# Shorter ways for the softmax sums and the heads' rows, two more score blocks and a new written-out order in a gated attention and mixer block

## The chip, the core and the metric

The kernel runs on one core of a Trainium2 chip. A core has a matrix engine (TensorE, PE in the profile; its weight loads, PEld, are listed apart), a vector engine (VectorE, DVE), a scalar engine that evaluates functions (ScalarE, ACT), a general engine (GpSimd, POOL), and a synchronising engine (SyncE, SP), on whose queue nearly all DMA transfers of this kernel are issued. The metric is the time of one execution in microseconds on the device.

## The reference, cut to what matters

There are 2048 tokens of 512 features. `a` is attention with 32 heads of 16 features and no mask; `b` is a mixer with a shift of the hidden rows and a wide MLP; a gate of each token mixes the two.

```python
g = _sigmoid((x * gate_w).sum(-1, keepdims=True))
qkv = (x @ wqkv).reshape(B, S, 3, H, Dh)          # H = 32, Dh = 16
p = _softmax(einsum(q, k) * (Dh ** -0.5))
a = einsum(p, v).reshape(B, S, D) @ wo
h = _gelu(_layernorm(x) @ w1)                     # quarters of h shifted by 1, -1, 2, -2 tokens
x1 = x + shifted(h) @ w2
b = x1 + _gelu(_layernorm(x1) @ w3) @ w4          # w3: 512 x 1792
return g * a + (1 - g) * b
```

All inputs are bf16. The largest part is the attention: 32 x 2048 x 2048 exponentials.

## The kernel before, in words

**Blocks and rounds.** The 2048 queries are cut into 4 chunks `c` of 512. The 32 heads are 4 groups `G` of 8; of these, 4 heads lie in the 4 row quarters of PE at once, the even ones in the first round (`p` = 0) and the odd ones in the second. So there are 4 x 4 x 2 = 32 rounds (`rounds`, L1497), each with 16 key tiles x 4 heads = 64 score blocks of 128 keys x 512 queries, 2048 blocks in all. A block is one matmul on a quarter of PE (L1536) into one of the 8 PSUM banks.

**Two ways to take an exponential.** Either ACT evaluates Exp on 2 or 3 blocks at once (L1631) and writes `prob`; or DVE does it on pairs of blocks. DVE multiplies and adds so that the 16 bits of the result, read as bf16, are a rough exponential (L1663), and then adds 32, 64 and 96 to these bits (`sh`, L1704): the four versions together give a good one. The additions run on DVE (L1706) or on POOL (L1708). A block of ACT's needs one value matmul (L1761), a block of DVE's four. The value matmuls have a column of ones beside the 16 value features, so that row 0 of each quarter of the sum is the softmax's denominator. `prob` has room for 56 blocks (`NPROB`, L908).

**End of a round.** `finish_round` (L1772) copies the sum to `accsb` (DVE, L1782), then sends its four rows of denominators to DRAM (`den`, L1784) and from there to `pk`, 16 to a partition (L1786), takes the reciprocal, multiplies by the gate's factor (L1789, L1790), writes it to DRAM (`rr`, L1792), and reads it back to all partitions in four transfers (`bcs`, L1796). POOL multiplies (`oT`, L1800). Four transfers then put the 16 rows of each head at their place in the group's buffer `oD` (L1804), in which both rounds of a group lie together. `oD` has 6 buffers of 512 columns, `oT` two. The matmuls with `wo` (loaded in one piece, L1091) run at the end of the MLP's last product (`w4`, L1447 to L1455). The very last round is finished apart, behind L2122.

**MLP.** Its products run between the score blocks in groups of column quarters (`gen`, L1127). A normalised tile is made on POOL (L1358), stored to DRAM (`xn_dram`, L1362) and read back transposed (L1368).

**The start.** x's first four tiles come on two queues, then the first query weights (`wq`, L1051) on SP and the first key weights on ACT's queue, then x's second chunk in one piece of 512 KB (L1053), the first value weights (L1054), and transposed chunks of x (L1060). PE warms up with 9 matmuls, transposes the first chunk (L1206) and projects it (L1198); the second chunk is transposed on PE later (L1165).

**What sets the order.** Nothing is scheduled on the chip. The class `Sim` runs a model of the five engines while the kernel is built: each step is a `Job` with a duration (`hold`), a latency, dependencies, buffers that it takes and frees, and a priority; SP's transfers are jobs too (`dma`, L1009). The times at which the model starts the jobs give the order in which the instructions are written out (L2116), and each engine then follows that order and waits on semaphores. Its choices depend on some 40 settings, `BASE`, that a table `STEPS` overwrites for each stretch of 8 score blocks, 256 stretches in all. Some of them: `GP2`, the share of DVE's pairs that have two additions on POOL and not one; `GP3`, one minus the share of pairs with all three on DVE; `DVE_WAIT`, how many blocks may wait for DVE; `DVE_STOP`, at how many blocks left in a round DVE gets no more; `CAP3`, up to how many banks ACT's blocks may hold for three to be taken together.

Of the kernel before, what the change touches and what calls it, by code (L numbers as in the profile page):

```python
# [191 lines left out]
class Sim:  # L192
# [6 lines left out]
    def __init__(self, slots):  # L199
# [24 lines left out]
        self.readers = {}  # L224
        self.usable = [0.0] * 8
# [108 lines left out]
    def try_engine(self, e):  # L334
# [136 lines left out]
def kernel(  # L471
# [77 lines left out]
        0: dict(P1_PRIO=0.312, GP2=0.15, DVE_STOP=8, DVE_STOP_L=12, DVE_ALONE=138, SL0=-150, SL1=130, IDLE_NS=864,  # L549
            BRES=2, AHEAD=16, PV_FULL=0.947, PV_IDLE=0.25, PRESS=22, ROT=1, AT_SH=118, HOLE=3, CAP3=5, LIMD=4, GATE=4,  # L550
            AFIRST=1, LIMA=2, JOIN=1),
        1: dict(P1_PRIO=0.743, S_PRIO=0.178, DVE_STOP_L=7, URG=2, DVE_ALONE=-158, SL0=45, SL1=0, PV_IDLE=0.731,
            E_PRIO=0.25, JOIN=2),
        2: dict(ROT=3, E_PRIO=2, ROWM=7),
        3: dict(P1_PRIO=0.414, S_PRIO=0.625, GP2=0.8, DVE_STOP_L=16, URG=3, DVE_ALONE=2, SL0=0, B_LOW=5, DVE_WAIT=2,
            AHEAD=24, AHEAD2=32, PV_IDLE=0.5, MAXU=3, DUE_SH=-6, AT_SH=69, MAXG=2, CAP3=0, LIMD=3, GATE=3, E_PRIO=0.25,
            AGE=6000, ROWM=3, JOIN=0),
        4: dict(GP2=1, EARLY=64, SL1=-150),
        5: dict(P1_PRIO=0.743, S_PRIO=0.3, DVE_STOP=2, DVE_STOP_L=7, URG_L=18, DVE_ALONE=362, SL1=60, B_LOW=8, BRES=4,
            AHEAD2=24, PV_FULL=0.916, PV_IDLE=0.25, PRESS=18, MAXU=2, ROT=2, HOLE=7, MAXG=1, CAP2=5, CAP3=7, AFIRST=2,  # L560
            AGE=9000, ROWM=99, LIMA=3),
        6: dict(P1_PRIO=0.312, S_PRIO=0.214, DVE_STOP=13, DVE_STOP_L=16, URG_L=12, DVE_ALONE=2, B_LOW=3, BRES=0,
            DVE_WAIT=1, AHEAD2=32, PV_FULL=1, PV_IDLE=0.117, ROT=0, DUE_SH=-14, HOLE=0, MAXG=3, GATE=4, AFIRST=1,
            AGE=3000, JOIN=1),
        7: dict(S_PRIO=0.38, E_PRIO=2, AGE=12000),
# [620 lines left out]
    def first(t):  # L1186
# [45 lines left out]
        for k in range(KT):  # L1232
            j_xT[0, 0, k] = at_time(t + 2100.0)
# [538 lines left out]
    def finish_round(r):  # L1772
# [35 lines left out]
        if r == NR - 2:  # L1808
            packs.extend(d4)
# [366 lines left out]
```

## Time and profile before

| | |
|---|---|
| median of 3 runs | 731.45 us (731.16 to 733.74) |
| the profiled execution | 731.34 us, of which the span of instructions is 729.4 |
| granted clock of TensorE | 1.0 |
| busy: PE, DVE, ACT, POOL | 719.9, 698.0, 713.2, 481.0 us |
| DMA | 38.27 MB, mean 52 GB/s |

How to read a group: line of the kernel, engine, operation, tile written <- tile read, shapes, count | busy time in us, mean duration in ns | idle time of the engine just before, and what ended it. Durations of neighbours overlap on an engine, so that the busy time of a group is less than count x mean. A row of a stretch has its two ends, then for PE, PEld, DVE, ACT and POOL the busy us with the number of instructions in brackets, the first figure being the stretch's length. A row of one line of the kernel gives the shortest, median and longest duration in ns and the first and last start. In a list of waits there are the waiting engine and line, what it waited for, the us in total, how often, and the longest.

### The profile page before, as it was taken

How to read it: one execution, taken by the hardware profiler on the slowest of the kernel's cores; microseconds unless marked ns; L12 is line 12 of the kernel's file. 1: busy time of each engine (PE TensorE's matmuls, PEld its weight loads, DVE VectorE, ACT ScalarE, POOL GpSimd, SP SyncE). 2: the span in 40 equal slices, each digit the busy share in tenths (PEclk: the TensorE clock that was granted, in tenths of full speed). 3: DMA queues.
4: the chain of work that ended last, by engine and by line, in shares of the span. 5: the costliest groups of instructions: out<-in, count | busy, mean ns of one | idle time of the engine just before them, and what ended most of it. 6: DMA issues, size and time to landing. Idle time of an engine off the chain costs nothing.

```text
span 729.4 us, 23745 instructions
## 1 busy us (share of the span) xinstructions
PE 719.9 (99%) x9533; PEld 214.3 (29%) x9533; DVE 698.0 (96%) x1461; ACT 713.2 (98%) x728; POOL 481.0 (66%) x502
## 2 busy tenths in 40 slices
PE   9999999999999999999999999999999999999997
PEld 5334322232332222223222222222222232222222
DVE  6999899999999999999999999999999999999997
ACT  6999989999999999999999999999999999999995
POOL 2786767778786876685556556686777856564451
PEclk9999999999999999999999999999999999999999
DMA  9222422323123210141111101221100131000001
GB/s 188 79 61 54 101 71 46 65 50 89 61 67 79 59 41 22 45 137 53 24 26 35 28 22 29 63 80 28 41 19 21 36 102 26 25 28 21 18 19 40
DMA packets 69543, 38.27 MB, mean 52 GB/s; under 512 B 46893, under 2 KB 64317, under 8 KB 69433
## 3 DMA queue, kind: packets, MB, share of 16 engines
q1 hardware_dynamic: 68472, 36.23, 19.7%
q8 instruction: 74, 1.21, 0.7%
q10 hardware_dynamic: 960, 0.52, 0.3%
q14 instruction: 37, 0.29, 0.2%
HBM read 21.07 MB, written 6.81 MB: 38 GB/s over the span
## 4 chain that ended last, share of the span: by engine, by line
PE 80%; ACT 13%; DVE 2%; issue 2%; DMA 1%; POOL 1%; SPq 0%; ACTq 0%; DVEq 0%
PE banks L1761 29%; PE banks L1536 26%; PE banks L1134 24%; ACT prob L1631 12%; ACT hT L1378 1%; DVE prob L1706 1%; DMA wq<-in_A_wqkv_dram 1%; DMA xn_dram<-xn 1%; DVE prob L1663 0%; PE banks L2111 0%; POOL prob L1708 0%; ACT L1378 0%; DVE hB L1431 0%; PE banks L1291 0%; PE banks L1198 0%
## 5 line engine op out<-in xcount | busy, mean ns | idle before, releaser
L1631 ACT ACTIVATE prob<-banks 128x1024 bf16<-128x1024 f32 (+1 forms) x705 | 669.1, 1121 | 3.1 <-PE banks L1536 2.8
L1708 POOL TENSOR_SCALAR prob<-prob 128x1024 uint16<-128x1024 uint16 x364 | 374.5, 1047 | 180.7 <-DVE prob L1706 118.5
L1663 DVE TENSOR_SCALAR prob<-banks 128x512 uint16<-128x512 f32 (+1 forms) x577 | 385.0, 693 | 12.7 <-PE banks L1536 8.0
L1761 PE MATMUL banks<-prob,V 128*17 128x512 bf16 (+1 forms) x3818 | 319.6, 381 | 2.1 <-POOL prob L1708 1.5
L1536 PE MATMUL banks<-q,kT 32*128 32x512 bf16 x2048 | 275.7, 384 | 1.4 <-ACT prob L1631 0.2
L1706 DVE TENSOR_SCALAR prob<-prob 128x1024 uint16<-128x1024 uint16 x521 | 192.3, 423 | 3.6 <-POOL prob L1708 2.3
L1536 PEld LDWEIGHTS <-kT 32*128 32x128 bf16 x2048 | 69.1, 90 | 289.0 <-ACT prob L1631 265.5
L1761 PEld LDWEIGHTS <-V 128*17 128x17 bf16 (+1 forms) x3818 | 73.5, 88 | 120.0 <-issue 96.4
L1134 PE MATMUL banks<-xnT,w 128*32 128x512 bf16 x1152 | 92.1, 383 | 0.0
L1800 POOL TENSOR_TENSOR oT<-accsb,bcs 128x512 bf16<-128x512 f32 x31 | 39.5, 1275 | 28.8 <-DVE prob L1706 24.8
L1134 PE MATMUL banks<-w,hT 128*32 128x512 bf16 x696 | 57.6, 383 | 0.0
L1134 PEld LDWEIGHTS <-w 128*32 128x32 bf16 x1904 | 40.3, 95 | 48.3 <-issue 28.1
L1134 PE MATMUL banks<-w,w 128*32 128x256 bf16 (+1 forms) x752 | 38.0, 309 | 0.0
L1134 PE MATMUL banks<-w,hB 128*32 128x512 bf16 x448 | 37.7, 382 | 0.0
L1358 POOL TENSOR_SCALAR xn<-x_sb,rs,nm 128x512 bf16<-128x512 bf16 x32 | 25.0, 785 | 13.8 <-DVE prob L1706 3.7
L1145 PE MATMUL banks<-w,oD 32*128 32x512 bf16 x56 | 21.5, 384 | 0.0
L1338 DVE BATCH_NORM_STATS2 st<-x_sb 128x6 f32<-128x512 bf16 x32 | 21.4, 680 | 0.0
L1782 DVE COPY accsb<-banks 128x512 f32<-128x512 f32 x31 | 21.1, 680 | 0.1
L1134 PE MATMUL banks<-w,oD 128*32 128x512 bf16 x184 | 21.0, 384 | 0.1
L1134 PEld LDWEIGHTS <-hT 128*32 128x32 bf16 x696 | 14.9, 95 | 19.9 <-issue 14.0
L1134 PE MATMUL banks<-w,wq 128*32 128x512 bf16 x240 | 19.8, 383 | 0.0
L1378 ACT ACTIVATE hT<-hT 128x7168 bf16<-128x7168 bf16 (+1 forms) x3 | 19.4, 6452 | 0.0
(100 smaller groups left out, 273.6 us busy)
## 6 DMA issues: line engine op xcount, KB each, us to landing
bcs<-rr SPq DMA_DIRECT2D x124, 64.0 KB
xn_dram<-xn SPq DMA_DIRECT2D x32, 128.0 KB
w<-in_B_w_dram SPq DMA_DIRECT2D x8, 512.0 KB
w<-in_B_w_dram SPq DMA_DIRECT2D x8, 448.0 KB
oD<-oT SPq DMA_DIRECT2D x124, 16.0 KB
x_sb<-in_A_x_dram SPq DMA_DIRECT2D x3, 512.0 KB
out_dram<-ot SPq DMA_DIRECT2D x12, 128.0 KB
w<-in_A_wqkv_dram SPq DMA_DIRECT2D x2, 256.0 KB
```

Source lines behind the costliest of these rows:

```text
L1134: units.append([Op("col", j, lambda j=j, lf=lf, rf=rf, n0=n0, n1=n1, st=st, sp=sp: nc.tensor.matmul(get()[32 * j:32 * j + 32, n0:n1], lhsT ...
L1145: o = Op("row", i, lambda: nc.tensor.matmul(get(), lhsT=lf(0, P)[rows], rhs=rf()[rows], start=False, stop=True, tile_position=(32 * i, 0), ...
L1338: a = dve(600, deps, lambda: nc.vector.bn_stats(out=sb.slot[:], in_=x_sb[:, t, :]), prio=6, at=at, acq=[sb])
L1358: g = gp(750, [m], lambda t=t, xb=xb: nc.gpsimd.tensor_scalar(out=xb.slot[:], in0=x_sb[:, t, :], scalar1=rs[which][:, t:t + 1], scalar2=nm ...
L1378: g = nc.scalar.activation(out=ap, in_=ap, func=ACT.Gelu_apprx_tanh)
L1536: o = Op("row", i, lambda: nc.tensor.matmul(dst(), lhsT=kT[G][32 * i:32 * i + 32, kt * P:(kt + 1) * P], rhs=qbuf[G, c].slot[32 * i:32 * i ...
L1631: job = act(hold, ops, lambda: nc.scalar.activation(out=prob[:, pb.cut(), :].bitcast(BF16), in_=unit()[:, rb.cut(), :], func=ACT.Exp, scal ...
L1663: return nc.vector.tensor_scalar(out=prob[:, b0.cut() if w == 2 else b0.bufs[h0].slot, :], in0=unit()[:, rb.cut() if w == 2 else rb.bufs[0 ...
L1706: return nc.vector.tensor_scalar(out=cut(k), in0=cut(0), scalar1=float(SHIFT * k), scalar2=None, op0=ALU.add)
L1708: return nc.gpsimd.tensor_scalar(out=cut(k), in0=cut(0 if both else 2), scalar1=1.0, scalar2=float(SHIFT * (k if both else 1)), op0=ALU.mu ...
L1761: return nc.tensor.matmul(one(accs[r])[32 * i:32 * i + n, :], lhsT=lhs(n), rhs=rhs(), start=st and not edge, stop=True, tile_position=(0, ...
L1800: n = gp(1250, d3, lambda: nc.gpsimd.tensor_tensor(out=ob.slot[:], in0=ab.slot[:], in1=bb.slot[:], op=ALU.mult), acq=[ob], frees=[ab, bb], ...
```

## The change

- The row sums go from `accsb` to `pk` in one transfer within SBUF; `den` is gone.
- Of each round but the last two, `oT` is stored whole, in one transfer of 128 KB, to a new DRAM array `o_dram`. When both rounds of a group are stored, one load brings the group's 128 rows of heads into `oD`. `oD` has four buffers and not six. The round before the last keeps its four direct transfers, with other places.
- In `oD` the even heads' rows now lie ahead of the odd ones', and `wo` is loaded in eight pieces so that its rows have the same order.
- `prob` has room for 58 blocks.
- x's second chunk on SP waits for the landing of the first query weights. All later transfers of the start stand behind it on that queue.
- One warm-up matmul fewer; two of the start's copies change between ACT and DVE.
- The model holds SP back while eight transfers are in flight (`sent`), and some of its durations are other ones.
- The whole table `STEPS` is a new one, so that the order of all engines is new. Over the 256 stretches the mean of `GP2` goes from 0.537 to 0.562, of `GP3` from 0.863 to 0.856, of `DVE_WAIT` from 3.00 to 2.67, of `DVE_STOP` from 7.37 to 6.52, of `CAP3` from 1.63 to 1.29.

```diff
@@ class Sim
+        self.sent = [0.0] * 8
...
+            land = max(self.t + 0.65 * (j.hold + j.lat), min(end, self.queue + 1500.0))
+            self.sent = self.sent[1:] + [land]
+            if self.sent[0] > self.t_free[e]:
+                self.t_free[e] = self.sent[0]
+                self.push(self.t_free[e], None)
@@ STEPS
-        0: dict(P1_PRIO=0.312, GP2=0.15, DVE_STOP=8, DVE_STOP_L=12, DVE_ALONE=138, SL0=-150, SL1=130, IDLE_NS=864,
...
+        0: dict(P1_PRIO=0.1, S_PRIO=0.214, GP2=0.8, DVE_STOP=8, URG_L=18, DVE_ALONE=500, SL0=0, SL1=130, IDLE_NS=864,
...
-    NPROB, NTOK, NW = 56, 5, 6
+    NPROB, NTOK, NW = 58, 5, 6
...
+    o_dram = dpool.tile([4 * NCH, 2, P, 512], BF16, name="o_dram")
...
-        "oD": slots("oD", 6, [P, 512]),
+        "oD": slots("oD", 4, [P, 512]),
...
-        "den": slots("den", 3, [4, 512], F32, dpool),
...
-        fn(nc.sync if eng == "SP" else nc.scalar)
+        insts.append(fn(nc.sync if eng == "SP" else nc.scalar))
         return job
+
+    insts = []
+
+    def behind(inst, first):
+        tc.add_manual_dep(inst.ins, first.ins.name, mybir.DependencyInfo(
+            mybir.DependencyClass.Sync, mybir.DependencyReason.DATA), reason="load order")
...
-    j_x1 = [start("SP", 4900.0, lambda q: q.dma_start(out=x_sb[:, 4:8, :], in_=x_src(1, 0, 4)))]
+    issue["SP"] = 5400.0
+    j_x1 = [start("SP", 2900.0, lambda q: q.dma_start(out=x_sb[:, 4:8, :], in_=x_src(1, 0, 4)))]
+    behind(insts[-1], insts[4])
...
-    wload("o", A_wo, 10 ** 6)
-    dl_w["o"].at = 855
+    bo = wslot("o", 10 ** 6)
+    for n in range(8):
+        G, p = n // 2, n % 2
+        dl_w["o"] = dma(3000.0, [], lambda G=G, p=p: nc.sync.dma_start(
+            out=bo.slot[64 * p:64 * p + 64, G, :],
+            in_=A_wo[G * P:(G + 1) * P, :].rearrange("(j p i) c -> p j i c", p=2, i=16)[p]), acq=[] if n else [bo], prio=2)
...
-        for _ in range(9):
+        for _ in range(8):
...
-                cp = nc.scalar.copy if i in (1, 3) else nc.vector.tensor_copy
+                cp = nc.scalar.copy if i == 2 else nc.vector.tensor_copy
...
-            sim.readers[ba] = [nc.vector.tensor_copy(out=kT[0][:, 0:256], in_=one(ba)[:, 0:256])]
+            sim.readers[ba] = [nc.scalar.copy(out=kT[0][:, 0:256], in_=one(ba)[:, 0:256])]
...
-                in_=zE_dram[S - 512:S].rearrange("(b e) -> e b", e=32)), prio=6)
+                in_=zE_dram[S - 512:S].rearrange("(b e) -> e b", e=32)), prio=6).at = 300 + 20 * j
...
-            wdeps = [dl_w["o"]] + j_att[c][:2 * ng]
+            wdeps = [dl_w["o"]] + j_att[c][:ng]
...
+        for G in range(4 if c < NCH - 1 else 3):
+            j_att[c].append(dma(3300.0, [att_done[c * 8 + 2 * G], att_done[c * 8 + 2 * G + 1]], lambda c=c, G=G: nc.sync.dma_start(
+                out=oDbuf[c, G].slot[:], in_=o_dram[4 * c + G].rearrange("p (j q) n -> (p j) q n", q=32)[:, 1:DH + 1, :]),
+                acq=[oDbuf[c, G]], prio=1))
...
-        d0 = dma(2000.0, [e], lambda: nc.sync.dma_start(out=db.slot[:], in_=ab.slot[0:P:32, :]), prio=1, acq=[db],
-                 frees=[ab], hold=580.0)
-        d1 = dma(2800.0, [d0], lambda: nc.sync.dma_start(
-            out=kb.slot[:], in_=db.slot[:].rearrange("j (b e) -> (j b) e", e=16)), prio=1, acq=[kb], frees=[db],
-            hold=400.0)
+        d1 = dma(2600.0, [e], lambda: nc.sync.dma_start(out=kb.slot[:], in_=ab.slot[0:P:32, :]), prio=1, acq=[kb],
+                 frees=[ab], hold=570.0)
...
+        fin = Call(lambda: sim.set_done(att_done[r]))
+        if r < NR - 2:
+            dma(2900.0, [n], lambda: nc.sync.dma_start(out=o_dram[4 * c + G, p], in_=ob.slot[:]), frees=[ob, fin], prio=1,
+                hold=400.0)
+            return
         d4 = []
         for j in range(4):
...
-                out=oDbuf[c, G].slot[32 * j + 16 * p:32 * j + 16 * p + 16, :], in_=ob.slot[32 * j + 1:32 * j + DH + 1, :]),
...
+                out=oDbuf[c, G].slot[64 * p + 16 * j:64 * p + 16 * j + 16, :], in_=ob.slot[32 * j + 1:32 * j + DH + 1, :]),
```

More of the change, by code (lines that the diff above doesn't have):

```diff
@@ L558 @@
[L558 to L564, printed above, removed]
@@ L1833 @@
             PLAN["w4", 4 * c + t] = int(a + (b - a) * t / 4)
[L1835 removed]
+    first(3480.0)
     begun = [j_ka[0], j_q[0, 0, 0]]
```

730 lines of the change are left out of this document (366 added, 364 removed).

## The prediction

> **What bounds the kernel now.** I read the page's busy shares and its chain first, then the groups by shape, then busy time by stretch, and last the timeline of the one stretch that stands out. The busy shares:
>
> ```profile
> PE 719.9 (99%) x9533; PEld 214.3 (29%) x9533; DVE 698.0 (96%) x1461; ACT 713.2 (98%) x728; POOL 481.0 (66%) x502
> PE 80%; ACT 13%; DVE 2%; issue 2%; DMA 1%; POOL 1%; SPq 0%; ACTq 0%; DVEq 0%
> ```
>
> Three engines look full. The stretches tell them apart (columns: time, then busy us and instructions of PE, weight loads, DVE, ACT, POOL, the granted clock, the DMA share, GB/s):
>
> ```profile
> 0.00:10.00 10.00, 8.26 (x63) 5.53 (x63) 4.32 (x13) 4.51 (x7) 3.88 (x14) 1.00 0.92 195
> 60.00:88.00 28.00, 28.00 (x488) 10.89 (x484) 27.04 (x57) 28.00 (x29) 18.99 (x22) 1.00 0.40 90
> 88.00:90.00 2.00, 1.55 (x26) 0.31 (x15) 0.44 (x2) 2.00 (x3) 2.00 (x3) 1.00 0.13 42
> 90.00:94.00 4.00, 2.92 (x35) 0.94 (x34) 2.46 (x10) 2.24 (x3) 0.86 (x2) 1.00 0.20 55
> 94.00:120.00 26.00, 25.90 (x342) 7.10 (x340) 25.20 (x47) 25.33 (x28) 22.28 (x24) 1.00 0.20 55
> 94.00:715.00 621.00, 619.45 (x8046) 173.76 (x8047) 606.40 (x1250) 619.93 (x634) 418.51 (x425) 1.00 0.17 46
> 360.00:480.00 120.00, 119.88 (x1556) 31.43 (x1547) 117.98 (x250) 119.98 (x132) 73.69 (x73) 1.00 0.15 42
> 715.00:730.00 15.00, 10.07 (x93) 3.23 (x86) 8.92 (x20) 6.81 (x9) 1.57 (x2) 1.00 0.12 40
> ```
>
> From 94 to 715 us ACT is idle 1.07 us in 621 and DVE 14.6. So there is no repeated wait to remove: ACT's exponentials are the bound, and DVE, which takes part of the score blocks off ACT, has 2.4% left. ACT's idle time lies at the start (5.5 us of the first 10), at the end (8.2 from 715 on), and in one place between: 1.76 us in 90 to 94 and 0.67 in 94 to 120, 2.43 together, with 3.1 us of DVE's in 88 to 94. All of ACT's from 88 to 715 is 1.76 + 1.07 = 2.83.
>
> The division of the score blocks, by shape (count, then busy time and mean duration):
>
> ```profile
> L1631 ACT ACTIVATE prob<-banks 128x1024 bf16<-128x1024 f32 x657 | 614.0, 1089 | 2.9 <-PE banks L1536 2.7
> L1631 ACT ACTIVATE prob<-banks 128x1536 bf16<-128x1536 f32 x48 | 74.0, 1550 | 0.2 <-PE banks L1536 0.2
> L1708 POOL TENSOR_SCALAR prob<-prob 128x1024 uint16<-128x1024 uint16 x364 | 374.5, 1047 | 180.7 <-DVE prob L1706 118.5 <-PE banks L1761 20.8 <-PE banks L1536 13.2
> L1663 DVE TENSOR_SCALAR prob<-banks 128x512 uint16<-128x512 f32 x564 | 369.5, 681 | 12.2 <-PE banks L1536 7.7 <-issue 0.3 <-PE banks L1761 0.2
> L1706 DVE TENSOR_SCALAR prob<-prob 128x1024 uint16<-128x1024 uint16 x521 | 192.3, 423 | 3.6 <-POOL prob L1708 2.3 <-PE banks L1761 0.4 <-DVE prob L1706 0.2
> L1663 DVE TENSOR_SCALAR prob<-banks 128x1024 uint16<-128x1024 f32 x13 | 15.9, 1220 | 0.5 <-PE banks L1536 0.3
> ```
>
> ACT does 657x2 + 48x3 = 1458 blocks, DVE 564 + 26 = 590, together the 2048. A block on ACT costs 688.0/1458 = 0.47 us. A pair on DVE costs 2 x 385.4/590 = 1.31 us and its shifts: 521 + 364 = 885 = 3 x 295, so 1.77 of three on DVE at 192.3/521 = 0.37 us, 0.65 together. One pair moved from ACT to DVE thus frees ACT 0.94 us and costs DVE 1.96.
>
> **The change, part by part.** The terms are summed against the profiled execution, 731.34 us (span 729.4), which stands 0.11 under the median of the runs, 731.45.
>
> *Start.* x's second chunk (512 KB on SP) now waits until the first query weights have landed, and everything behind it on SP waits too.
>
> ```profile
> 1.68 4.56 DMA wq<-in_A_wqkv_dram
> 2.17 0.58 SPq L1053 DMA_DIRECT2D x_sb<-in_A_x_dram  x1
> 3.97 1.91 PE L1206 MATMUL banks<-idb,x_sb 128*128 128x128 bf16 x16
> 6.28 0.61 PE L1198 MATMUL banks<-w,wq 128*128 128x256 bf16 x4 [0.39 <-DMA wq<-in_A_wqkv_dram]
> 8.78 5.97 ACT L1631 ACTIVATE prob<-banks 128x1536 bf16<-128x1536 f32 x5 [0.17 <-PE banks L1536]
> 9.13 1.07 PE L1165 MATMUL banks<-idb,x_sb 128*128 128x128 bf16 x16
> ```
>
> PE ends the transposes at 5.88 and starts projecting at 6.28, after 0.39 us of waiting for the weights. That wait is all that a faster landing can give. I take half, -0.2, as the weights still share the DMA engines with the first key weights. The other end: the chunk is issued at 6.24 instead of 2.17; with a flight as long as the weights' 4.56 it lands at 6.24 + 0.58 + 4.56 = 11.4, while PE transposes it from 9.13. PE takes its work in order, so the scores behind would be late by 2.3; ACT's five exponentials, 5.97 us from 8.78, cover most of that. Ends -0.4 and +2.3. One warm-up matmul fewer and the copies moved between ACT and DVE end before the weights' landing, or in place of one another: nothing.
>
> *Row sums and heads' rows.* Per round, two hops of the sums become one and four transfers of the rows become one; per pair of rounds one load is added.
>
> ```profile
> L1784 SPq DMA_DIRECT2D den<-accsb x31: 499/532/1032, 38.6 to 701.8; - x31
> L1786 SPq DMA_DIRECT2D pk<-den x31: 326/341/576, 40.4 to 703.5; - x31
> L1804 SPq DMA_DIRECT2D oD<-oT x124: 508/587/1626, 79.6 to 717.4; - x124
> L1134 PE MATMUL banks<-w,oD x184: 376/379/392, 330.5 to 716.6; 128*32 128x512 bf16 x184
> ```
>
> Removed are 31 hops and 30 x 3 row transfers, added 15 loads and 7 for the split output weights: 99 transfers fewer. By these rows SP issues for about 31 x 0.34 + 90 x 0.59 - 22 x 0.59 = 50 us less, and a round's reciprocal can come 40.4 - 38.6 = 1.8 us sooner. The rows now make a trip to DRAM and back, two flights of some 4.2 us for one. What hides both is the distance of the output projection, which in before starts only at 330 us for rows finished from 80 us on. With four buffers for them instead of six, a finished chunk waits in DRAM and holds no oT. So away from the stall below I cost these at nothing; uncovered, the added flight is 4.2 us a chunk. The last pair keeps its four direct stores, so the end is unchanged.
>
> *The stall at 88 to 94 us.* Its timeline and the chain there:
>
> ```profile
> 83.40 4.17 DMA xn_dram<-xn
> 84.47 2.41 SPq L1804 DMA_DIRECT2D oD<-oT  x4
> 86.98 0.54 SPq L1784 DMA_DIRECT2D den<-accsb  x1
> 87.66 2.02 POOL L1358 TENSOR_SCALAR xn<-x_sb,rs,nm 128x512 bf16<-128x512 bf16 x2 [1.15 <-DMA xn_dram<-xn]
> 89.65 1.04 POOL L1708 TENSOR_SCALAR prob<-prob 128x1024 uint16<-128x1024 uint16 x1
> 90.73 0.43 DVE L1706 TENSOR_SCALAR prob<-prob 128x1024 uint16<-128x1024 uint16 x1 [2.29 <-POOL prob L1708]
> 91.97 0.25 DVE L1789 RECIPROCAL pk<-pk 128x16 f32<-128x16 f32 x1 [0.81 <-DMA pk<-den]
> ```
>
> POOL's normalisation waits for a store in flight; the shift queued behind it on POOL is late; DVE waits 2.29 us for that and then 0.81 for a row sum's second hop; PE and ACT follow. Both transfers that bracket it are in the part that is cut, and the planner now also holds SP back when eight transfers are in flight, so a new order would place such stores where they come in time. I take the whole of ACT's loss here, -2.4. The other end is a second stall of that size, +2.4: it is the only one in 705 us, and a new order can have its own. Late next is the gate's own chain, which does not change.
>
> *Two more score blocks, new settings.* The order of all five engines is planned anew. Averaged over the 256 stretches of the table (each setting holds until it is overwritten), GP2, the share of pairs with a second shift on POOL, goes from 0.537 to 0.562, and GP3, one minus the share with all on DVE, from 0.863 to 0.856. Shifts on DVE per pair, 3(1 - GP3) + GP3(2 - GP2), fall from 1.67 to 1.66: 0.011 x 295 x 0.37 = 1.2 us less on DVE, of which 0.94/(0.94 + 1.96) reaches the time: -0.4; I take -0.3. By the Trainium skill's page SBUF — State Buffer, Who interferes with whom, a GpSimd instruction and a DVE one in a two-port mode exclude each other on a shared port pair, which speaks against this term; the trace agrees as far as POOL's 118.5 us of waiting on L1706 goes, and by the rule the sum would be 0.3 higher.
>
> For the rest: DVE has 14.6 us in 94 to 715, and used up entirely that is 14.6/(1.96 + 0.94) = 5.0 pairs, 4.7 us. I take the row of 360 to 480, where the same planner leaves DVE 1.7% idle: with that everywhere, 10.5 us would be left, so 4.1/2.90 x 0.94 = -1.3. Ends -4.7 and zero, or worse if the new order is the poorer one (below). Width of the exponentials: CAP3, which allows three blocks, falls from 1.63 to 1.29 on average; 0.51 us a block busy in the wide ones against 0.47 says a gain, 0.52 against 0.54 by duration a loss; nothing taken.
>
> Sum: 731.34 - 0.2 - 2.4 - 0.3 - 1.3 = 727.1; against the median, 727.2.
>
> **Rivals.** *A: no change.* The stall comes back as a similar one, and the new order packs no better; only the start and the shifts are left, 731.45 - 0.2 - 0.3 = 730.9. For it: outside the stall ACT has 0.4 us of idle time from 88 to 715 to give back, and the removed transfers end no other wait. Against it: DVE's spare 14.6 us.
>
> *B: slower, by the division of work.* The new order gives DVE fewer pairs. DVE_WAIT, the blocks that may wait for DVE, falls from 3.00 to 2.67 on average, and DVE starves wherever a block comes late, with ACT doing the rest at 0.94 us a pair. Ten pairs of the 295 cost 9.4: 727.2 + 9.4 = 736.6. It decides at 4.5 pairs; slower by 0.5% begins at 8.4. Against it: DVE_STOP, the rest of a round at which DVE gets no more, falls too (7.4 to 6.5), which gives DVE more.
>
> *C: PE bounds.* If PE's 80% of the chain were its own work, pairs moved to DVE, which need eight matmuls after the exponential where ACT's need two, would cost instead of help, and the -1.3 goes: 728.5. Against it: before 640 of the scores' groups the weight loads wait for ACT, 265.5 us in all.
>
> ```profile
> PEld L1536 <- ACT prob L1631: 265.5, 640, 0.6
> ```
>
> By the Trainium skill's page Perfetto Trace Analysis, Identifying the Most-Contended Engine, matmul busy time is a poor measure of how full PE is, and the weight loads' share a better one. The trace agrees, with 29% beside 99%; by that rule C falls away.
>
> **How the numbers follow.** 0.5% of the time, 3.7 us, is about what a measurement tells from no change: faster is below 727.8, slower above 735.1. The forecast has 0.50, with a range of its own from 723.5 to 729.5, of which 0.41 lies below 727.8; all bounds of gain together give 731.45 - 0.4 - 2.4 - 0.4 - 4.7 = 723.5. A has 0.16. C has 0.07, of which 0.03 is below 727.8. B has 0.27, of which 0.25 is over 735.1 and some 0.10 over 737.5, since lost pairs add up with a second stall or the late chunk. So faster 0.44, same 0.31, slower 0.25. The range from 723 to 737.5 leaves out about 0.05 below and 0.10 above.
>
> **What would show it.** Start: PE's first projection waits under 0.2 us for wq, and the first exponential starts by 8.6; wrong if the transposes of the second chunk wait for x_sb. Stall: ACT's idle time between 88 and 715 us falls from 2.83 to under 1; wrong if POOL's normalisation still waits for xn_dram. Division: 296 to 298 pairs, shifts on DVE at or below 1.77 a pair, DVE idle 10 us; with fewer than 291 pairs B holds. Rows: the output projection waits for no oD load, and accsb's copy for no buffer. The prediction is wrong above all if ACT has as little idle time as I say and more than 1458 blocks.

## The result, and the profile after

The changed kernel takes 728.49 us (median of 8 runs, 727.93 to 730.26), the kernel before 731.77 beside it (8 runs, 729.75 to 733.74): a ratio of 0.9956, with a 95% interval of 0.9941 to 0.9971. That is 3.3 us less, just inside the 0.5% that the prediction called no change. The profiled execution took 728.68 us, its span 725.9; before, 731.34 and 729.4. So the span fell by 3.5 us and the time by 2.7: what lies outside the span grew from 1.94 to 2.78.

The busy shares of the changed kernel, from its page:

```profile
PE 716.5 (99%) x9560; PEld 215.2 (30%) x9561; DVE 700.4 (96%) x1467; ACT 712.8 (98%) x729; POOL 478.4 (66%) x501
```

Busy time by stretch after, with the columns of the prediction's (PE, weight loads, DVE, ACT, POOL, granted clock, DMA share, GB/s):

```profile
0.00:10.00 10.00, 7.97 (x58) 5.02 (x59) 5.09 (x14) 5.44 (x8) 3.87 (x14) 1.00 0.62 171
10.00:60.00 50.00, 49.62 (x829) 20.40 (x830) 48.55 (x112) 49.10 (x47) 34.48 (x39) 1.00 0.39 96
88.00:94.00 6.00, 5.88 (x96) 2.01 (x88) 6.00 (x16) 5.90 (x8) 1.73 (x3) 1.00 0.20 51
94.00:120.00 26.00, 25.82 (x349) 7.33 (x345) 25.08 (x50) 26.00 (x29) 20.05 (x21) 1.00 0.25 50
94.00:712.00 618.00, 615.44 (x8036) 174.16 (x8032) 603.67 (x1245) 617.55 (x635) 415.87 (x422) 1.00 0.19 51
```

The one stall is gone: ACT loses 0.10 us in 88 to 94 and nothing in 94 to 120; before, it lost 2.43 in the two together. From 94 to 712 it loses 0.45 us in all. Something came in, though. From 10 to 60 ACT loses 0.90 us. Before, the same stretch reads so:

```profile
10.00:60.00 50.00, 49.69 (x808) 19.67 (x809) 48.40 (x114) 49.75 (x49) 35.14 (x39) 1.00 0.39 83
```

That was a loss of 0.25. The groups by shape after (count, then busy time and mean duration, then idle time before):

```profile
L1652 ACT ACTIVATE prob<-banks 128x1024 bf16<-128x1024 f32 x659 | 614.5, 1096 | 0.4
L1652 ACT ACTIVATE prob<-banks 128x1536 bf16<-128x1536 f32 x47 | 72.4, 1540 | 1.1 <-PE banks L1557 1.1
```

and DVE's and POOL's:

```profile
L1684 DVE TENSOR_SCALAR prob<-banks 128x512 uint16<-128x512 f32 x575 | 375.9, 681 | 11.9 <-PE banks L1557 7.0
L1684 DVE TENSOR_SCALAR prob<-banks 128x1024 uint16<-128x1024 f32 x7 | 8.5, 1219 | 0.4 <-PE banks L1557 0.3
L1727 DVE TENSOR_SCALAR prob<-prob 128x1024 uint16<-128x1024 uint16 x519 | 192.2, 425 | 2.2 <-PE banks L1782 1.3 <-issue 0.2 <-PE banks L1557 0.2
L1727 DVE TENSOR_SCALAR prob<-prob 128x512 uint16<-128x512 uint16 x3 | 0.7, 288 | 0.0
L1729 POOL TENSOR_SCALAR prob<-prob 128x1024 uint16<-128x1024 uint16 x363 | 372.7, 1045 | 187.8 <-DVE prob L1727 131.3 <-PE banks L1782 16.1 <-PE banks L1557 11.7
```

ACT does 659 x 2 + 47 x 3 = 1459 blocks (1458 before), DVE 575 + 7 x 2 = 589 (590 before). The 589 are 294 pairs and one block alone, which has its three shifts on DVE at half the width. The shifts are 519 + 3 + 363 = 885, as before, and 522 of them are on DVE (521 before), that is 1.77 of three, as before. The division of the work has moved by one block.

The start and the end, from the timeline after:

```profile
5.28 0.38 SPq L1064 DMA_DIRECT2D x_sb<-in_A_x_dram  x1
5.31 0.61 PE L1216 MATMUL banks<-w,wq 128*128 128x256 bf16 x4
7.81 3.71 ACT L1652 ACTIVATE prob<-banks 128x1536 bf16<-128x1536 f32 x3 [0.17 <-PE banks L1557]
9.64 1.07 PE L1183 MATMUL banks<-idb,x_sb 128*128 128x128 bf16 x16
711.54 6.02 ACT L1652 ACTIVATE prob<-banks 128x1536 bf16<-128x1536 f32 x5
718.04 0.72 DVE L2140 STREAM_TRANSPOSE accsb<-banks 128x512 f32<-128x512 f32 x1
```

and the end before:

```profile
708.90 11.64 ACT L1631 ACTIVATE prob<-banks 128x1536 bf16<-128x1536 f32 x12
719.78 1.05 POOL L1708 TENSOR_SCALAR prob<-prob 128x1024 uint16<-128x1024 uint16 x1 [4.25 <-ACT prob L1631]
721.50 0.72 DVE L2122 STREAM_TRANSPOSE accsb<-banks 128x512 f32<-128x512 f32 x1 [1.60 <-PE banks L1761]
```

The first exponential starts at 7.81 and not at 8.78, since PE's first projection starts at 5.31 and not at 6.28; from there to the exponential it takes 2.50 us in both. The last exponential ends at 711.54 + 6.02 = 717.56, and 8.34 us of the span follow; before it ended at 720.54, with 8.86 us behind it. There the last pair's shift on POOL (1.05 us) is still to come when ACT is nearly done, and the closing transposition waits 1.60 us; in the new order that shift runs on DVE and the transposition waits for nothing.

So the 3.5 us of span are made up of: first exponential earlier, 0.97; shorter tail, 0.52; ACT's idle time between 88 us and the end of the score blocks down from 2.83 to 0.10 + 0.45 = 0.55, 2.28; and against these 0.65 more of idle time from 10 to 60. That makes 3.12. The other 0.38 is ACT's own work (its busy time fell from 713.2 to 712.8) and rounding. Outside the span 0.84 is lost again. This compares one execution with one; a second execution of the changed program, told of at the end of the experiments, has its first exponential at 8.14.

One wait of the old stall is still there, in small:

```profile
POOL xn L1376 <- DMA xn_dram<-xn: 0.8, 2, 0.5
```

POOL's normalisation waits twice for a store, at 75 and at 83 us, and ACT loses nothing there (it is busy for all 28 us from 60 to 88).

### The profile page after: what moved, and what is told of

The parts are those of the page before. It is cut to its first block, busy times and chain, and to the rows that moved or that the text cites. A ratio compares the mean times of both kernels' runs of the same rounds, so it can differ in the third digit from the quotient of the medians.

```text
span 725.9 us, 23600 instructions
## 1 busy us (share of the span) xinstructions
PE 716.5 (99%) x9560; PEld 215.2 (30%) x9561; DVE 700.4 (96%) x1467; ACT 712.8 (98%) x729; POOL 478.4 (66%) x501
## 4 chain that ended last, share of the span: by engine, by line
PE 82%; ACT 9%; DVE 6%; issue 2%; POOL 1%; ACTq 0%; POOLq 0%; DVEq 0%
PE banks L1782 29%; PE banks L1557 27%; PE banks L1152 25%; ACT prob L1652 8%; DVE prob L1684 2%; DVE prob L1727 2%; POOL prob L1729 1%; ACT hT L1396 1%; DVE st L1356 0%; PE banks L1131 0%; PE banks L2129 0%; DVE accsb L1803 0%; PE banks L1224 0%; PE banks L1216 0%; ACT L1398 0%
## 5 line engine op out<-in xcount | busy, mean ns | idle before, releaser
L1729 POOL TENSOR_SCALAR prob<-prob 128x1024 uint16<-128x1024 uint16 x363 | 372.7, 1045 | 187.8 <-DVE prob L1727 131.3
L1782 PE MATMUL banks<-prob,V 128*17 128x512 bf16 (+1 forms) x3815 | 315.0, 381 | 0.5 <-POOL prob L1729 0.3
L1152 PE MATMUL banks<-w,hT 128*32 128x512 bf16 x688 | 62.3, 383 | 0.0
L1163 PE MATMUL banks<-w,oD 32*128 32x512 bf16 x52 | 20.0, 384 | 0.0
L1449 DVE CAST hB<-banks 128x512 bf16<-128x512 f32 x28 | 18.8, 678 | 0.5 <-PE banks L1152 0.5
```

Source lines behind the costliest of these rows:

```text
L1152: units.append([Op("col", j, lambda j=j, lf=lf, rf=rf, n0=n0, n1=n1, st=st, sp=sp: nc.tensor.matmul(get()[32 * j:32 * j + 32, n0:n1], lhsT ...
L1729: return nc.gpsimd.tensor_scalar(out=cut(k), in0=cut(0 if both else 2), scalar1=1.0, scalar2=float(SHIFT * (k if both else 1)), op0=ALU.mu ...
L1782: return nc.tensor.matmul(one(accs[r])[32 * i:32 * i + n, :], lhsT=lhs(n), rhs=rhs(), start=st and not edge, stop=True, tile_position=(0, ...
```

## Experiments

All are timed beside the kernel before on the same chip. "Changed" and "before" say which kernel an experiment starts from. Spans are medians over the runs; the views, and the numbers read from them, are of one profiled execution each. In experiments that start from the kernel before, its order of instructions on the engines stays, so that the edit alone is seen.

### The wait of x's second chunk, undone in the changed kernel

```diff
     j_x1 = [start("SP", 2900.0, lambda q: q.dma_start(out=x_sb[:, 4:8, :], in_=x_src(1, 0, 4)))]
-    behind(insts[-1], insts[4])
```

> The changed kernel, without the second chunk's wait for the query weights; the order of all engines is the same. My account of the two traces: the wait is why the weights land at about 5.2 us and not at 6.2, so without it the first projection starts at 6.2 to 6.3 and the first exponential at about 8.7 (7.81 with it). The second chunk is then early, so that the 0.65 us which ACT loses between 10 and 60 us in the changed kernel come back: span +0.2 to +0.9 us. Rival (the weights land earlier for another reason, such as the order of the first transfers on the two queues): first exponential within 0.1 us of 7.81, span within 0.3 us. The prediction's step had 0.2 us for the wait.

Measured: 729.58 us, ratio 0.9975 [0.996, 0.999]; span 727.1. Its timeline at the start, and its stretch from 10 to 60:

```profile
6.04 0.61 PE L1215 MATMUL banks<-w,wq 128*128 128x256 bf16 x4 [1.02 <-DMA wq<-in_A_wqkv_dram]
8.53 3.71 ACT L1651 ACTIVATE prob<-banks 128x1536 bf16<-128x1536 f32 x3 [0.17 <-PE banks L1556]
10.00:60.00 50.00, 49.58 (x811) 20.21 (x811) 48.68 (x113) 49.11 (x46) 33.75 (x39) 1.00 0.39 88
```

Without the wait the query weights come 0.7 us later, and PE waits for them again (1.02 us). Beside the next experiment, which has the wait and ran on the same chip, the wait is worth 0.9 us, in the span and in the time. ACT's new loss from 10 to 60 is the same 0.9 us with and without the wait. So it isn't the price of the later chunk, for which it had been taken before the run; it belongs to the new order.

### Nine warm-up matmuls in the changed kernel

```diff
-        for _ in range(8):
+        for _ in range(9):
```

> The changed kernel with nine warm-up matmuls in place of eight, order unchanged. My account: x's first tile has landed by 3.5 us, so the ninth matmul holds the transposes back: they start at about 3.97 and not 3.65, and with the weights there at 5.2 the projections and the first exponential come 0.3 us later, span +0.2 to +0.3. Rival, the prediction's step (the matmul costs nothing, since the weights' landing comes after it): first exponential unchanged.

Measured: 728.64 us, 0.9963 [0.9948, 0.9978]; span 726.2.

```profile
3.98 1.33 PE L1224 MATMUL banks<-idb,x_sb 128*128 128x128 bf16 x16
5.23 0.61 PE L1216 MATMUL banks<-w,wq 128*128 128x256 bf16 x4
```

The transposes start 0.3 us later than after eight warm-ups (3.65) but take 1.33 us where the changed kernel's sixteen take 1.69, and the projection begins no later (5.23 against 5.31), nor does the first exponential (7.72 against 7.81). How long the transposes take differs from execution to execution: a second one of the changed program has 1.33 us from 3.66 on. So no cost of the ninth matmul is seen at the start, as the prediction had it. The median span is 726.2, against 725.9 and 726.05 in two measurements of the changed program, not beside it, so that up to 0.3 us can't be excluded.

### The wait alone, in the kernel before

```diff
     j_x1 = [start("SP", 4900.0, lambda q: q.dma_start(out=x_sb[:, 4:8, :], in_=x_src(1, 0, 4)))]
+    behind(insts[-1], insts[4])
```

> The kernel before, with the second chunk's wait alone; order unchanged. My account: the weights land by 5.3 us, the projections then wait for the transposes (end 5.88) and their copies, first projection at 5.9 to 6.0 (6.28 before), first exponential at 8.4 to 8.5 (8.78); the second chunk is issued 3 us later, and its transposes start at 9.6 to 10 (9.13), which PE's order passes on. Span -0.4 to +0.5. The prediction's far end has the chunk at 11.4 and +2.3.

Measured: 731.74 us, 1.0 [0.9986, 1.0013]; span 729.9 (before: 729.7).

```profile
5.56 0.37 SPq L1059 DMA_DIRECT2D x_sb<-in_A_x_dram  x1
5.59 0.61 PE L1205 MATMUL banks<-w,wq 128*128 128x256 bf16 x4 [0.23 <-DVE w L1218]
8.09 2.37 ACT L1638 ACTIVATE prob<-banks 128x1536 bf16<-128x1536 f32 x2 [0.17 <-PE banks L1543]
9.69 1.05 PE L1172 MATMUL banks<-idb,x_sb 128*128 128x128 bf16 x16 [1.33 <-DMA x_sb<-in_A_x_dram]
10.00:60.00 50.00, 49.69 (x806) 19.72 (x803) 48.17 (x113) 48.80 (x48) 34.71 (x39) 1.00 0.39 88
```

Here is the collision that the prediction bounded at +2.3. The weights come earlier and the first exponential moves up by 0.7 us, but PE now waits 1.33 us for the chunk, and ACT loses 1.20 us from 10 to 60 where it lost 0.25. Gain and loss cancel. In the old order the transposes of the second chunk stand right behind the first six score matmuls (0.71 us of PE). In the new order eleven come first, and at 9.64 the chunk is there.

### The whole new start, in the kernel before

The wait, eight warm-ups, and both copies that change engines.

```diff
+    behind(insts[-1], insts[4])
...
-        for _ in range(9):
+        for _ in range(8):
...
-                cp = nc.scalar.copy if i in (1, 3) else nc.vector.tensor_copy
+                cp = nc.scalar.copy if i == 2 else nc.vector.tensor_copy
...
-            sim.readers[ba] = [nc.vector.tensor_copy(out=kT[0][:, 0:256], in_=one(ba)[:, 0:256])]
+            sim.readers[ba] = [nc.scalar.copy(out=kT[0][:, 0:256], in_=one(ba)[:, 0:256])]
```

> The kernel before, with all of the new start: wait, eight warm-up matmuls, the copies moved between ACT and DVE; the rest of the order unchanged. My account: first exponential at 7.8 to 7.9 as in the changed kernel, -0.9 to -1.0, of which the late second chunk takes back some 0.3 to 0.7 by 60 us, as there: span -0.2 to -0.7. Rival (the new order is needed for an earlier start to be worth anything): span within 0.2 of the kernel before or above it.

Measured: 731.26 us, 0.9998 [0.9986, 1.0011]; span 729.4.

```profile
9.57 1.05 PE L1172 MATMUL banks<-idb,x_sb 128*128 128x128 bf16 x16 [1.42 <-DMA x_sb<-in_A_x_dram]
```

The first exponential starts at 7.88, but PE has the same wait, 1.42 us, ACT loses 1.29 us from 10 to 60, and no gain is left.

### Four real buffers for the first layer norm's tile, in the kernel before

POOL's normalisation waited for a store that still read its buffer. This takes away its reason: in the first layer norm four different parts of a tile that is free by then (`hB`) take turns.

```diff
-            g = gp(750, [m], lambda t=t, xb=xb: nc.gpsimd.tensor_scalar(
-                out=xb.slot[:], in0=x_sb[:, t, :], ...
+            real = (lambda xb=xb: xb.slot[:]) if which else (lambda t=t: hB[:, (t % 4) * 512:(t % 4 + 1) * 512])
+            g = gp(750, [m], lambda t=t, real=real: nc.gpsimd.tensor_scalar(
+                out=real(), in0=x_sb[:, t, :], ...
```

> The kernel before, with four buffers in place of two for the normalised tiles of the first layer norm (they lie in the space of hB, which is free until later); order unchanged. POOL's write of the next tile no longer waits for a store to land. My account: the stall at 88 to 94 us begins with that wait, so ACT's idle time there (1.76 us, and 0.67 up to 120) goes almost whole: span -1.7 to -2.4. Rival (the stall is made by the row sum's second hop, for which DVE waits 0.81 us, and by POOL being late anyway): span -0.8 or less.

Measured: 731.21 us, 1.0 [0.9988, 1.0012]; span 729.4 (before: 729.5).

```profile
84.71 2.41 SPq L1805 DMA_DIRECT2D oD<-oT  x4
86.28 2.19 POOL L1359 TENSOR_SCALAR hB<-x_sb,rs,nm 128x512 bf16<-128x512 bf16 x2
87.23 0.54 SPq L1785 DMA_DIRECT2D den<-accsb  x1
89.68 0.43 DVE L1707 TENSOR_SCALAR prob<-prob 128x1024 uint16<-128x1024 uint16 x1 [0.93 <-POOL prob L1709]
91.98 0.25 DVE L1790 RECIPROCAL pk<-pk 128x16 f32<-128x16 f32 x1 [1.88 <-DMA pk<-den]
```

POOL waits no more, and DVE's wait for POOL falls from 2.29 to 0.93 us. But its wait for the row sums grows from 0.81 to 1.88, and the reciprocal comes at the same time as before (91.98 for 91.97). ACT loses 2.68 us from 86 to 120, where it lost 2.43. So two waits ran side by side, and the store was not the one that set the end. In front of the row sums' first hop, on SP, stand the four row transfers with 2.41 us.

### Row sums in one transfer, in the kernel before

The single transfer within SBUF is issued where the second hop stood; the first hop is gone.

```diff
-        d0 = dma(2000.0, [e], lambda: nc.sync.dma_start(out=db.slot[:], in_=ab.slot[0:P:32, :]), prio=1, acq=[db],
+        d0 = dma(2000.0, [e], lambda: None, prio=1, acq=[db],
...
-            out=kb.slot[:], in_=db.slot[:].rearrange("j (b e) -> (j b) e", e=16)), prio=1, acq=[kb], frees=[db],
+            out=kb.slot[:], in_=ab.slot[0:P:32, :]), prio=1, acq=[kb], frees=[db],
```

> The kernel before, with the row sums in one transfer within SBUF, issued where the second hop stood; the first hop is left out, the rest of the order unchanged. SP then has 31 transfers fewer, and the sums land no later than before. Rival of my account (the removed hop is what ends the stall at 88 to 94 us): span -0.8 to -2.4. My account (the sums are off the path everywhere but for 0.81 us inside the stall): span within 0.8 us, most likely -0.3.

Measured: 730.16 us, 0.9985 [0.9975, 0.9994]; span 728.4, which is 1.1 less than before beside it.

```profile
90.16 1.73 POOL L1358 TENSOR_SCALAR xn<-x_sb,rs,nm 128x512 bf16<-128x512 bf16 x2 [1.08 <-DMA xn_dram<-xn]
92.94 0.43 DVE L1706 TENSOR_SCALAR prob<-prob 128x1024 uint16<-128x1024 uint16 x1 [2.45 <-POOL prob L1708]
93.51 0.25 DVE L1789 RECIPROCAL pk<-pk 128x16 f32<-128x16 f32 x1
```

The first exponential of this execution starts 2.1 us later than before's (10.84), so its stall lies later too. The reciprocal no longer waits for its sums; DVE still waits 2.45 us for POOL, and POOL for the store. Taking away either wait leaves the other; the one taken away here was the one that ended last. ACT's loss from 86 to 120 is 1.91 us here. Of the 1.1 us of span this trace shows 0.5, and even that is not sure: with nothing changed but the start, the same stretch loses 2.73 us in one execution (the wait alone) and 1.52 in another (the whole new start).

### Heads' rows stored whole, in the kernel before

One store per round to DRAM in place of four transfers, a load once both rounds are stored, `wo` in eight pieces, in all four chunks. Only the last pair of rounds keeps its direct way.

```diff
+        def rows(j):
+            if r == NR - 2:
+                nc.sync.dma_start(out=oDbuf[c, G].slot[64 * p + 16 * j:64 * p + 16 * j + 16, :], ...
+            elif j == 0:
+                nc.sync.dma_start(out=o_dram[4 * c + G, p], in_=ob.slot[:])
+
+        def load():
+            sim.emit(sim.t + 1000.0, lambda: nc.sync.dma_start(out=oDbuf[c, G].slot[:], in_=o_dram[4 * c + G]...
```

> The kernel before, with the heads' rows stored whole and loaded back per pair, 1 us after the model has the last of them done, wo loaded in eight pieces; still six buffers and 56 blocks, order of PE, DVE, ACT and POOL unchanged. The prediction costs this at nothing away from the stall: span within 0.3 us. Rival (the four row transfers between the stores of normalised tiles cause the stall): POOL's wait at 87 us is shorter and the span -1 to -2.4.

Measured: 731.48 us, 1.0011 [0.9998, 1.0025]; span 729.65. The timeline at the old stall and late in the last chunk:

```profile
83.94 0.52 SPq L1793 DMA_DIRECT2D den<-accsb  x1
90.36 0.24 DVE L1798 RECIPROCAL pk<-pk 128x16 f32<-128x16 f32 x1
702.57 0.63 SPq L1821 DMA_DIRECT2D oD<-o_dram  x1
705.53 0.40 PE L1143 MATMUL banks<-w,oD 128*32 128x512 bf16 x4 [1.19 <-DMA oD<-o_dram]
706.30 6.63 ACT L1640 ACTIVATE prob<-banks 128x1536 bf16<-128x1536 f32 x6 [1.03 <-PE banks L1545]
```

and ACT's loss by stretch:

```profile
86.00:94.00 8.00, 7.90 (x104) 2.41 (x103) 8.00 (x20) 7.47 (x8) 5.28 (x7) 1.00 0.21 59
94.00:120.00 26.00, 26.00 (x356) 7.33 (x352) 25.20 (x49) 25.93 (x29) 21.15 (x22) 1.00 0.21 56
660.00:712.00 52.00, 50.81 (x662) 13.90 (x662) 49.63 (x108) 50.96 (x55) 25.74 (x25) 1.00 0.09 26
```

The stall shrinks from 2.43 to 0.60 us although the row sums still go in two hops: without the four transfers in front of it the first hop is issued at 83.94, not 86.98. In this stretch POOL's normalisation and DVE's reciprocal no longer wait for a transfer, though neither the stores of normalised tiles nor the two hops were edited. That names the root: SP was held for 2.41 us by the rows, and all that stood behind them, sums and stores alike, came late. In the last chunk the same edit costs: the load is issued at 702.57 for a projection that starts at 703.55, PE waits 1.19 us for it, and ACT loses 1.04 us from 660 to 712, where it lost nothing. The prediction's cover for the second flight holds for three chunks and is missing in the fourth. By these two numbers the span should be 0.8 us shorter, and its median is not; the rest stays open.

### The last shift on DVE, in the kernel before

```diff
+                on_pool[0] += 1
+                if on_pool[0] == 364:
+                    return nc.vector.tensor_scalar(out=cut(k), ..., op0=ALU.add)
```

> The kernel before, with the last of the 364 shifts on POOL done by DVE instead, at the same place of the written order. My account of the two ends: the last value matmuls wait for that shift (719.78 to 720.83 us), 1.05 us on POOL against 0.42 on DVE, so the end comes 0.4 to 0.7 us sooner, as it does in the changed kernel, where the last shifts are DVE's. Rival (the end is set by the last exponential): within 0.1 us.

Measured: 731.14 us, 1.0001 [0.9989, 1.0014]; span 729.2 (before: 729.5).

```profile
714.67 6.55 ACT L1631 ACTIVATE prob<-banks 128x1024 bf16<-128x1024 f32 x7
721.78 0.72 DVE L2128 STREAM_TRANSPOSE accsb<-banks 128x512 f32<-128x512 f32 x1 [0.84 <-PE banks L1767]
```

The span behind the last exponential is 729.7 - 721.22 = 8.48 us, 0.38 less than before's 8.86. That is most of the 0.52 that the changed kernel gains there, and too little to be seen in the time.

### Sums, rows and last shift together, in the kernel before

The three edits before, with the sums issued at the first hop's place and the last chunk's rows still sent directly.

```diff
-        d0 = dma(2000.0, [e], lambda: nc.sync.dma_start(out=db.slot[:], in_=ab.slot[0:P:32, :]), prio=1, acq=[db],
+        d0 = dma(2000.0, [e], lambda: nc.sync.dma_start(out=kb.slot[:], in_=ab.slot[0:P:32, :]), prio=1, acq=[db],
...
+            if c == NCH - 1:
+                nc.sync.dma_start(out=oDbuf[c, G].slot[64 * p + 16 * j:64 * p + 16 * j + 16, :], ...
```

> The kernel before in its old order, with three edits: row sums in one transfer within SBUF, issued where the first hop stood; heads' rows stored whole and loaded back for chunks 0 to 2 alone, chunk 3 direct (its load was waited for when all four went through DRAM); the last shift on POOL done by DVE. My account by now: the stall at 88 to 94 us has two waits side by side, POOL's for a store and DVE's for the second hop, both late because the four row transfers hold SP; with SP free both go. ACT's idle time from 86 to 120 us at most 0.6 (2.43 before), no wait for a load of oD, the end 0.4 us nearer to the last exponential: span 2 to 2.8 below the kernel before, that is within 0.8 to 1.6 us of the changed kernel, without a new order. Rival (the new order and its settings make the gain): span within 1 us of the kernel before.

Measured: 729.27 us, 0.9979 [0.9966, 0.9992]; span 727.5 (before: 729.2).

```profile
86.00:120.00 34.00, 33.45 (x450) 9.60 (x447) 32.27 (x67) 33.14 (x36) 27.24 (x28) 1.00 0.22 61
```

The old order with these edits has 1.7 us less of span. ACT's loss from 86 to 120 is 0.86 us, and no projection waits for a load of `oD`. The gain is less than was expected (a span 2 to 2.8 us shorter, a loss of at most 0.6), and more than the 1 us that the rival allowed, which gave the whole gain to the new order.

### The same with the new start

```diff
+    behind(insts[-1], insts[4])
```

and the other lines of the new start, on top of the last kernel.

> The same with the new start added (wait, eight warm-up matmuls, the moved copies). My account: in the old order the second chunk's transposes stand behind the first six score matmuls on PE, so that what the earlier first exponential gains (0.9 us) is lost by 20 us: median span within 0.4 us of the kernel without the new start, but a narrower spread of runs, as in the changed kernel (725.5 to 726.3 there, 726.5 to 728.4 without the wait). Rival (the wait is worth 1.2 us in any order): 0.8 to 1.2 below it.

Measured: 729.25 us, 0.998 [0.9971, 0.999]; span 727.45. The median does not move (727.5 without). The spans lie from 726.5 to 728.0, against 726.8 to 729.3 without the new start; but the 729.3 is a single run, and the other eleven end at 728.0 too. So in the old order the start gives nothing here either, and a narrower spread is not shown.

### The old table on the new structure

The changed kernel, with the settings of the kernel before (`BASE` and `STEPS`) and planned anew.

```diff
-        0: dict(P1_PRIO=0.1, S_PRIO=0.214, GP2=0.8, DVE_STOP=8, URG_L=18, DVE_ALONE=500, SL0=0, SL1=130, IDLE_NS=864,
+        0: dict(P1_PRIO=0.312, GP2=0.15, DVE_STOP=8, DVE_STOP_L=12, DVE_ALONE=138, SL0=-150, SL1=130, IDLE_NS=864,
...
```

> The changed kernel with the old table of settings, planned anew: new transfers, buffers, blocks and start, but an order that nobody chose for them. If the new table is what the gain needs: 731 to 745 us, with ACT's idle time between 20 and 700 us several us and not 0.5. Rival (the gain is in the transfers and the start, and any order will do): 727.5 to 730.

Measured: 790.17 us, 1.0803 [1.0772, 1.0834]. Busy time by stretch, and the waits of ACT:

```profile
94.00:120.00 26.00, 25.21 (x342) 9.81 (x340) 23.13 (x45) 17.87 (x19) 19.80 (x21) 1.00 0.27 63
120.00:712.00 592.00, 581.37 (x7220) 169.65 (x7212) 539.22 (x1069) 556.07 (x558) 367.19 (x374) 1.00 0.18 49
ACT prob L1654 <- PE banks L1559: 32.7, 32, 7.7
```

The old table doesn't fit the new structure. With it ACT loses 8.1 us in 94 to 120 and 35.9 in 120 to 712, with single waits for PE of up to 7.7 us. Against this the whole result of 3.3 us is small. The other two corners, the old structure with the new table and the new structure with 56 blocks, were not tried.

### The changed kernel without the limit of eight in flight

```diff
-            if self.sent[0] > self.t_free[e]:
+            if False and self.sent[0] > self.t_free[e]:
```

> The changed kernel planned with a model that does not hold SP back at eight transfers in flight; the table is the new one. The order changes wherever the model differs. If the limit describes the chip, transfers come later than this plan has them and ACT waits more: 729.5 to 735 us. Rival (the limit matters nowhere, or the plan hardly changes): within 0.7 us of the changed kernel's 728.5.

Measured: 728.46 us, 0.9972 [0.9961, 0.9984]; span 726.05. The program that comes out is the changed kernel's, instruction for instruction, so the limit does nothing here, and this is a second measurement of the change, beside other runs of the kernel before: 0.28% faster where the first gave 0.44%, with intervals that overlap.

Its start, in the one execution profiled:

```profile
5.64 0.61 PE L1216 MATMUL banks<-w,wq 128*128 128x256 bf16 x4 [0.65 <-DMA wq<-in_A_wqkv_dram]
```

The first exponential follows at 8.14. The same program thus waits for the query weights in one execution and not in the other.

No other program tried was faster than the changed one.

## Why the prediction came out as it did

The time, 728.49, lies 1.3 us over the 727.2 of the forecast and inside its own range of 723.5 to 729.5. The sum was nearly right, but not by its terms, and that is partly luck. Of its terms 1.6 us did not come, and what lies outside the span took 0.84 in the profiled execution; against that stand 0.52 at the tail and 0.38 of ACT's own work, neither of them forecast. Of the three outcomes it gave the best chance to "faster" (0.44), and the result lies in "no change" (0.31). And what it named as its sign of being wrong above all is there: ACT has as little idle time as it said (0.55 us from 88 us on, under 1) and more than 1458 blocks (1459). The way by which DVE was to take work off ACT is the part that failed.

**The stall** (predicted -2.4). Right in size: ACT's idle time behind 88 us fell by 2.28. Its reason was half right. The prediction told one chain: store, POOL, then the reciprocal for another 0.81. The store that POOL waited for is not one of the removed transfers, and POOL still waits for such stores in the changed kernel, 0.8 us in all; the prediction had called that a sign of being wrong. With its own buffers for POOL nothing was gained; with one hop less, 1.1 us of span. There were two waits side by side, and the root of both was SP, held by the four row transfers for 2.41 us. The prediction named the limit of eight in flight as a help; it changes no instruction's place.

**The start** (predicted -0.2, ends -0.4 and +2.3). The first exponential came 0.97 us sooner, more than the lower end allowed, and from 10 to 60 ACT loses 0.65 more: -0.32 net. The step that failed is "that wait is all that a faster landing can give". It took the end of PE's transposes, 5.88, as a floor, and that was the end in one execution: in the five other kernels profiled that start as before it lies between 5.15 and 5.88, and in the two executions of the changed program at 4.99 and 5.34. PE's wait for the weights in those that start as before is 0.39 to 1.72 us, but for the one told of in the last section. The other end, the late chunk, is real, but it needs the old order, in which it took the whole gain back. The wait pays only together with the later place of the second chunk's transposes.

**Row sums and rows away from the stall** (predicted nothing). Right for the changed kernel, in which no projection waits for `oD`. The sentence on its price, "uncovered, the added flight is 4.2 us a chunk", was put to the test by the old order with all four chunks stored whole: the last one stands uncovered and costs 1.0 to 1.2 us, since only part of the flight shows.

**Shifts and division** (predicted -0.3 and -1.3). Neither came. With 294 pairs and one block on DVE, 1459 blocks on ACT and 1.77 of three shifts on DVE, the new order divides the work as the old one did, and DVE's idle time from 94 us to the end of the score blocks is 14.3 us, as good as the 14.6 before. The step that failed is the reading of settings as results: means of `GP2`, `GP3` and the like over the table say little on what a planner makes of them (for the kernel before they gave 1.67 shifts a pair on DVE where the prediction's own count has 1.77), and that a stretch of 120 us had DVE 1.7% idle was no reason for the rest to follow. Without the two terms the sum would have been 731.45 - 0.2 - 2.4 = 728.85. By the Trainium skill's page SBUF — State Buffer, Who interferes with whom, a GpSimd instruction and a DVE one in a two-port mode exclude each other, which spoke against the term of the shifts. POOL's wait for DVE's shifts went from 118.5 to 131.3 us, which does not speak against that rule, but nothing here tells a wait for the port from a wait for the data.

**The tail** (predicted unchanged). It is 0.52 us shorter. The prediction looked at the four direct stores and not at the last pair's shift, which was on POOL, 1.05 us against 0.43 on DVE.

**Around the span** (not costed). The prediction summed against "its span and what lies around it" and let that stand. The time outside the span, as the median over the runs, is 1.81 to 1.86 us in before and 2.41 to 2.53 in the changed kernel and the three that differ from it in the wait, the warm-up matmul or the limit in flight. That takes back 0.6 us.

**The rivals.** A (no change, at 730.9) holds in one half: the new order packs no better. But the stall did not come back, and the result lies 2.4 us under its time. B (slower through fewer pairs) and C (PE as the bound) fell: DVE has one block fewer, and ACT lost 0.45 us in 618 while PE's loads filled 30%. The Trainium skill's page Perfetto Trace Analysis, Identifying the Most-Contended Engine, calls matmul busy time a poor measure for PE, and the trace agrees: PE at 99% did not keep ACT from being full.

**What the gain is made of.** In spans: the old order with sums, rows and last shift gives 1.7 us; the changed kernel gives 3.2 without the limit on what is in flight, beside the same runs of the kernel before, and 3.5 with nine warm-up matmuls. Of the rest 0.9 is the wait at the start in an order that fits it. In time, the new order without that wait (0.9975) is no better than the old order with the edits (0.9979); the wait, where it fits, is what sets the changed kernel apart. The remaining part of the span's gain, some 0.6 to 0.9, is about what goes outside the span. These are sums over different chips. What the new order, the 58 blocks and the four buffers are worth one by one was not tried.

## What to carry to other kernels

When an engine's wait is to be taken away, look for the second wait that ends at the same time, and follow both to the queue that they share; here several small transfers in front of a short, urgent one cost ACT more than the removal of either wait alone gave back. An edit to the loads and the place of their consumers in the order belong together: the same wait was worth 0.9 us in one order and nothing in another. And count the instructions that a planner put out, not the settings that it was given.

## What was not expected of the hardware

The landing of the first query weights depends on what is issued behind them on the same queue. With the 512 KB chunk, and with it all that follows it on SP, held back, PE's first projection started at 5.23 to 5.64 us in seven kernels profiled; with the chunk issued at about 2.2 us, at 6.04 to 6.87 in six, and in one at 5.33. In that one the first key weights were late instead, and PE waited for them before its second projection:

```profile
7.51 0.61 PE L1198 MATMUL banks<-w,w 128*128 128x256 bf16 x4 [1.43 <-DMA w<-in_A_wqkv_dram]
```

The mean DMA share of the first 10 us is 0.92 before and 0.87 in the changed kernel without the wait, and 0.62 with it. Whether it is the large chunk itself or the smaller transfers behind it is not shown, as the wait holds back both.

The spread of the time differs with it. Spans of the three kernels with the chunk held back in an order that fits lie within 1.0 us (725.5 to 726.5); without the wait within 1.9 (726.5 to 728.4), and the kernel before's within 4 to 5 (727.1 to 732.0). In the old order with the wait they lie within 2.2 (728.4 to 730.6).

The 0.6 us outside the span are open. They seem to come with the changed kernel's order or its buffers: the old order with sums, rows and the new start has 1.79, the changed kernel without the wait 2.41, and the old table on the new structure 2.10. What they are, no trace here shows, since a trace covers only the span.
